# The second product of both layers in seven products, and a new start of the attention stage

## The chip, the cores and the metric

The kernel runs on one NeuronCore of a Trainium2 chip, as one program. It uses five engines: TensorE (PE: matmuls; PEld is its weight load), VectorE (DVE), ScalarE (ACT), GpSimd (POOL) and SyncE (SP, which issues the DMAs). The metric is the device time of one execution in microseconds (us), the median of several runs, less is better. All arithmetic is float32; a matmul operand x is split in a rounded part hi (type fp32r) and a remainder lo = x - hi, and a product is made of three passes: hi·hi, hi·lo, lo·hi.

## What is computed

An attention over chunks of 64 tokens (4 batches, 8 heads, 576 tokens, 64 values per head), and its output through two layers:

```python
x = softmax(q_c @ k_c.T / 8) @ v_c           # in chunks of 64; x: 2304 tokens x 512
h = np.maximum(x @ w_in, 0.0)                # layer one, w_in 512 x 2048
x = (s * (h * h) + b) @ w_out                # w_out 2048 x 512, s and b scalars
h = x @ w2_in                                # layer two, same sizes
y = (np.maximum(h, 0) + np.log1p(np.exp(-np.abs(h)))) @ w2_out
```

The weights arrive as 64-bit floats, and the kernel makes 32-bit floats of them with integer instructions (function `convert`).

## The kernel before, in words

The 2304 tokens are 18 tiles of 128 (two tiles are a unit u, three units a group j; three groups of 768 tokens). Each matrix product is cut in 2 x 2 blocks over rows, columns and tokens. Three of the four big products are then made with seven block products instead of eight (Strassen's scheme in Winograd's form, numbered 1 to 7), for which sums of blocks of weights and of tokens ("forms") are made beforehand. A matmul here is 128 x 128 weights against 384 tokens (N = 384, half a group).

There are five stretches.
- Attention: per tile scores (L815), a maximum, exponentials, their sum, a scaling on POOL (L899), a transpose (L915) and the values (L934). The first `EARLY` = 6 tiles take their exponentials head by head on ACT (eight instructions, L839), the others in one (L874) with a subtraction and a sum on DVE. q, k and v of a tile lie in one of three places. While PE has nothing to do, it runs filler matmuls on zeros (L1502), a number fixed when the program is written.
- First product of layer one: `first_product` runs 24 quads (feature block i of 8, group j of 3), each of seven products of six matmuls (L1000). The products of a quad run through four accumulators in PSUM; between them ACT copies a partial sum to the next accumulator (`seed`, L1022) and DVE adds (L571). `hidden` (L1032) applies the relu on ACT, and the result goes to DRAM. The last two feature blocks come in the order `ENDING`, one after the other.
- Second product of layer one: `block`, six blocks (group, half), with all eight block products (L1179): 16 hidden blocks x 4 output blocks x 3 passes each. The hidden values are loaded again, squared on ACT (L1148), scaled by s and shifted by b (L436, L438), and split (L584, L593).
- First product of layer two: as for layer one, with Softplus; DVE then makes four sums per quad (L1080 to L1083) for the seven products that follow, and all seven forms are stored.
- Second product of layer two: `second_by_blocks`, seven products (L1335), product by product, and inside a product over the groups 2, 0, 1.

The order is set by a planner (`Work.order`): each operation is put down with the engines that may do it, a cost, a due key and what it depends on; the planner simulates the engines and always starts the operation that can start first, by key. A table TUNE shifts the keys. The instructions are emitted in that order, one fixed queue per engine. All DMAs go through SP's queue (`load`). Accumulators and buffers are `Place`s of a few kinds with a fixed number each.

## Time and profile before

| | us |
|---|---|
| median of three timed runs (808.88 to 811.23) | 809.07 |
| span of the profiled execution, first to last instruction | 805.9 |
| PE busy | 797.4 (99%) |
| PEld busy | 780.1 (97%) |
| DVE busy | 637.8 (79%) |
| ACT busy | 510.1 (63%) |
| POOL busy | 140.6 (17%) |
| DMA queue of SP, share of 16 engines' span | 66.9% |

The profiled execution has no time of its own beside its span; the median of the timed runs is 3.2 us longer than the span. Matmuls overlap: the length of one (some 335 ns) is not what it costs; that is the busy time of a full stretch divided by its matmuls. The mean length of a DVE or ACT instruction too includes an end that overlaps the next one's start when the engine has a backlog. The trace's mean granted TensorE clock is 0.999 of the full 2.4 GHz.

### The profile page before, as it was taken

What the parts mean: (1) busy time and instruction counts of PE and PEld (TensorE: products, weight loads), DVE (VectorE), ACT (ScalarE), POOL (GpSimd) and SP (SyncE); (2) the same over time, 40 slices, a digit from 0 to 9 for tenths busy, and PEclk for the clock granted to TensorE, in tenths of its full rate; (3) what the DMA queues carried; (4) which work ended last, traced back from release to release, by engine and by line L of the source; (5) the groups of instructions that cost most, each with busy time, mean ns of one, the idle gap of its engine ahead of it and who ended that gap; (6) DMA issues with size and microseconds to landing.
All of it is one profiled execution on the core that took longest, in us unless ns stands there. A gap on an engine that the chain in (4) does not pass through costs nothing.

```text
span 805.9 us, 14677 instructions
## 1 busy us (share of the span) xinstructions
PE 797.4 (99%) x5191; PEld 780.1 (97%) x5191; DVE 637.8 (79%) x1166; ACT 510.1 (63%) x1085; POOL 140.6 (17%) x162
## 2 busy tenths in 40 slices
PE   8999999999999999999999999999999999999998
PEld 6788999999999999999999999999999999999997
DVE  5999898988868978889946786898865777778864
ACT  5756866666658777776676764655555566555553
POOL 3444411111110112222212320213100000000000
PEclk9999999999999999999999999999999999999999
DMA  8865367878769666777540056766778997678851
GB/s 256 248 179 160 138 210 261 278 245 274 246 227 383 235 202 194 253 222 252 166 136 29 30 191 212 260 227 225 256 261 286 345 347 241 233 236 289 282 176 60
DMA packets 80634, 180.28 MB, mean 224 GB/s; under 512 B 9008, under 2 KB 53040, under 8 KB 79664
## 3 DMA queue, kind: packets, MB, share of 16 engines
q1 hardware_dynamic: 80560, 179.34, 66.9%
q8 instruction: 41, 0.67, 0.4%
q14 instruction: 33, 0.27, 0.1%
HBM read 111.15 MB, written 68.16 MB: 222 GB/s over the span
## 4 chain that ended last, share of the span: by engine, by line
PE 95%; DVE 3%; ACT 1%; issue 0%; POOL 0%; ACTq 0%; POOLq 0%; DVEq 0%
PE at L1000 20%; PE S L1000 13%; PE at L1179 9%; PE S L1179 9%; PE A L1000 9%; PE S L1335 8%; PE at L1335 8%; PE A L1179 6%; PE A L1335 5%; PE S L1502 2%; PE at L934 2%; PE at L815 1%; PE at L915 1%; DVE operands L593 1%; ACT last L839 0%
## 5 line engine op out<-in xcount | busy, mean ns | idle before, releaser
L571 POOL TENSOR_TENSOR mem<-mem 128x256 f32<-128x256 f32 x120 | 104.8, 883 | 377.6 <-DVE mem L551 279.9
L593 DVE TENSOR_TENSOR operands<-mem,operands 128x384 fp32r<-128x384 f32 (+4 forms) x186 | 126.3, 695 | 38.4 <-ACT operands L584 36.8
L593 DVE TENSOR_TENSOR operands<-last,operands 128x384 fp32r<-128x384 f32 (+2 forms) x184 | 111.2, 625 | 46.7 <-ACT operands L584 39.7
L584 ACT CAST operands<-mem 128x384 fp32r<-128x384 f32 (+4 forms) x186 | 111.7, 621 | 55.6 <-PE at L1335 36.0
L584 ACT CAST operands<-last 128x384 fp32r<-128x384 f32 (+2 forms) x184 | 93.5, 528 | 57.8 <-PE S L1179 23.1
L1000 PE MATMUL at<-operands 128*128 128x384 f32 x624 | 120.1, 336 | 0.4 <-ACT S L1022 0.4
L1000 PEld LDWEIGHTS at<-operands 128*128 128x128 f32 x624 | 109.4, 188 | 0.8 <-ACT S L1022 0.7
L1335 PE MATMUL at<-operands 128*128 128x384 f32 x384 | 87.2, 334 | 0.0
L1335 PE MATMUL S<-operands 128*128 128x384 f32 x384 | 87.2, 334 | 0.0
L1179 PE MATMUL at<-operands 128*128 128x384 f32 x432 | 84.5, 335 | 0.9 <-ACT operands L584 0.8
L1000 PE MATMUL S<-operands 128*128 128x384 f32 x420 | 83.6, 336 | 0.0
L1179 PE MATMUL S<-operands 128*128 128x384 f32 x432 | 83.1, 334 | 0.0
L1179 PEld LDWEIGHTS at<-operands 128*128 128x128 f32 x432 | 75.5, 188 | 1.9 <-ACT operands L584 1.1
L1032 ACT ACTIVATE mem<-S 128x384 f32<-128x384 f32 x104 | 51.0, 492 | 38.8 <-PE S L1000 29.3
L1179 PEld LDWEIGHTS S<-operands 128*128 128x128 f32 x432 | 75.6, 188 | 0.0
L1000 PEld LDWEIGHTS S<-operands 128*128 128x128 f32 x420 | 73.6, 188 | 0.3 <-issue 0.2
L571 DVE TENSOR_TENSOR mem<-mem 128x384 f32<-128x384 f32 (+1 forms) x108 | 61.0, 573 | 14.3 <-ACT mem L1032 10.8
L1335 PEld LDWEIGHTS S<-operands 128*128 128x128 f32 x384 | 68.4, 188 | 0.0
L1335 PEld LDWEIGHTS at<-operands 128*128 128x128 f32 x384 | 68.4, 188 | 0.0
L1000 PE MATMUL at<-last,operands 128*128 128x384 f32 x336 | 65.7, 335 | 0.0
L1000 PE MATMUL A<-operands 128*128 128x384 f32 x300 | 60.2, 339 | 0.4 <-DVE A L571 0.4
L1000 PEld LDWEIGHTS at<-last,operands 128*128 128x128 f32 x336 | 58.8, 188 | 0.0
(80 smaller groups left out, 1226.1 us busy)
## 6 DMA issues: line engine op xcount, KB each, us to landing
mem<-in_w_dram SPq DMA_DIRECT2D x64, 512.0 KB, 4.6
summed<-mem SPq DMA_DIRECT2D x168, 192.0 KB, 2.5
mem<-summed SPq DMA_DIRECT2D x30, 768.0 KB, 5.5
hid<-mem SPq DMA_DIRECT2D x96, 192.0 KB, 3.0
...
```

What stands on the lines that cost most here:

```text
L571: lambda e: on(e).tensor_tensor(out=out(), in0=x(), in1=y(), op=op or ALU.subtract),
L584: lambda e: nc.scalar.copy(out=hi().bitcast(F32R), in_=x()),
L593: lambda e: nc.vector.tensor_tensor(out=lo().bitcast(F32R), in0=x(), in1=hi(), op=ALU.subtract),
L815: nc.tensor.matmul(out_[c * D : (c + 1) * D, pr], of("q")[:, pr * P + c * D : pr * P + (c + 1) * D], kb[:, :, pr, c, :], start=True, stop= ...
L915: nc.tensor.transpose(at(pt)[:, c], of("e")[:, c], ident)
L934: nc.tensor.matmul(at(px)[y, x], of("v")[y, x], of("aT")[y, x], start=True, stop=True)
L1000: nc.tensor.matmul(acc(dst)().rearrange("p (u c) -> p u c", u=GROUP), l[a], r[c], start=start and kk == 0 and x == 0, stop=kk == 1 and x == 2,
L1032: lambda e: nc.scalar.activation(out=at(go), in_=acc(place)(), func=AF.Softplus if ph else AF.Relu),
L1179: nc.tensor.matmul(at(accs[d])[:, :N], l[a], r[c], start=m == 0 and z == 0, stop=m == NM - 1 and z == 2,)
L1335: nc.tensor.matmul(at(accs[d])[:, :N], l[a], r[c], start=i == 0 and y == 0, stop=i == NF - 1 and y == 2,)
L1502: nc.tensor.matmul(x, nought, nought.unsqueeze(1).to_broadcast([P, KK, P]), start=True, stop=True)
```

## The change

The second product of layer one is made in seven products too, by the same function as that of layer two (`second`), with the token groups outermost (2, 0, 1) and the products 1, 5, 6, 3, 7, 2, 4 inside a group. Four of the products run on in the accumulators of an earlier one (`GOES_ON`). Three of seven need sums of stored features; these are now made by DVE from loaded chunks, four feature blocks at a time (`summed_up`, 1536 elements per partition), in both layers, so that a quad stores four forms instead of seven (`FOUR`). The square moves to the quads (`squared`: ACT, or DVE straight from PSUM); s is applied when a result is read from PSUM, and b as a bias, b times the column sums of the weights, which come from two extra columns in three of the 21 steps of layer one. The weights' sums for the second product are made by POOL in `weights2` in both layers. All seven sets of weights are split once, during group 2, and kept in the SBUF.

In `convert`, layer one and the first weights of layer two take the sign and exponent through ACT (two Prelu instructions instead of one Relu; the first step on ACT or DVE) instead of one DVE instruction. The first six tiles of q, k and v have a place each, loads of the first four may be issued from ACT's queue, tiles 0, 1 and 3 alone take the head-by-head exponentials. The last two feature blocks are interleaved by group in both layers (`ENDING`). TUNE, some of the planner's costs and some keys change with it.

```diff
-EARLY = 6
+ENDING = [(i, j) for j in (2, 0, 1) for i in (NF - 2, NF - 1)]
+
...
+ORDER = 1, 5, 6, 3, 7, 2, 4
+GROUPS = 2, 0, 1
...
+GOES_ON = {2: 1, 3: 5, 7: 6, 4: 7}
+STAGE = 8, 7, 6, 5, 4, 3, *(8, 7, 6) * 4
+SLOTS = {"b": (3, 4), "t": (0, 1), "v": (2, 5), "u": (2, 5)}
+FIRST = SLOTS | {"b": (6, 7), "v": (3, 4)}
+GH, NGH = 896, 4
...
-            {"SP": 0.45},
+            {"SP": 0.55, "ACT": 0.6} if early else {"SP": 0.5},
             key,
-            lambda e: nc.sync.dma_start(out=out(), in_=in_()),
+            lambda e: (nc.scalar if e == "ACT" else nc.sync).dma_start(out=out(), in_=in_()),
...
+        leaky = ph == 0 or part == 0 and c < 4
...
+            elif e == "ACT":
+                nc.scalar.activation(
+                    out=a().bitcast(I32), in_=top(), func=AF.Identity, scale=1.0 / 16, bias=-15.0 / 32
+                )
...
+        o2 = add({"ACT": act(DM)}, key, scaled, [o1], [am])
+        o5 = add(
+            {"ACT": act(DM)} if leaky else {"DVE": dve(DM)}, key, signed, [o2], [am] if leaky else [f, am]
+        )
...
+        for o, l, r, op in ((4, 1, 3, ALU.add), (1, 0, 1, None), (5, 4, 0, None), (6, 2, 5, None)):
...
-        a = AT_X2 + t % 3 * XS
+        if t == 6:
+            another_use(2)
...
-        sc, pt, px = Place("at"), Place("at"), Place("at")
+        sc, pt, px = Place("A" if t < 6 else "at"), Place("at"), Place("at")
...
-            out_ = lambda: hid[ph][2 * j + half][:, 2 * i + row]
-            st = load(key + 0.1, out_, lambda: at(go), P * N * 4, [o], [go])
-            hid_in.setdefault((ph, j, half), []).append(st)
+
+            def squared(e):
+                if e == "DVE":
+                    nc.vector.tensor_tensor(out=at(go), in0=at(go), in1=acc(place)(), op=ALU.mult)
+                else:
+                    nc.scalar.activation(out=at(go), in_=at(go), func=AF.Square)
+
+            return go, add({"ACT": act(N), "DVE": dve(N, port=False)}, key, squared, [o], [place, go])
+
...
+        if FOUR[ph]:
+            o1 = sub(key, of(b12), of(b12), of(b11), N, [b12[1], b11[1]], [b12[0], b11[0]])
...
-    def block(ph, j, half, t0, first):
...
-            g, src = lambda x=x: mem(*x, 2 + 2 * ph), [ld]
-            if ph == 0:
-                o = add(
-                    {"ACT": act(N)},
-                    key - LEAD_H,
-                    lambda e, g=g: nc.scalar.activation(out=g(), in_=g(), func=AF.Square),
-                    [ld],
-                    w=[x],
-                )
...
-            for d in range(4):
...
-                    for z, (a, c) in enumerate(((0, 0), (0, 1), (1, 0))):
-                        nc.tensor.matmul(
...
-    def second_by_blocks(ph, t0):
...
+    def second(ph, t0):
...
+        steps = [(n, j) for j in GROUPS for n in ORDER]
...
+        summing = {(1, g0), (2, g0), (5, g0)} if ph == 0 else set()
...
+        def summed_up(x, y, z, key):
+
+            a, b, c = [(CHUNKS[w], CHUNK) for w in (x, y, z)]
+            sub(key, lambda: here(*a), lambda: here(*b), lambda: here(*c), CHUNK, (), r=[b, c], w=[a])
...
+
+                    def more(e, ps=ps, y=y):
+                        if ph:
+                            nc.vector.tensor_tensor(out=y(), in0=ps(), in1=y(), op=ALU.add)
+                        else:
+                            nc.vector.scalar_tensor_tensor(
+                                out=y(), in0=ps(), scalar=s_sb[:, 0:1], in1=y(), op0=ALU.mult, op1=ALU.add
+                            )
...
+                        elif e == "ACT":
+                            nc.scalar.activation(
+                                out=y(), in_=ps(), func=AF.Identity, scale=s_sb[:, 0:1], bias=bias[:, c : c + 1]
+                            )
...
+            if n in (1, 5, 6):
+                accs[n, j] = [Place({1: "at", 5: "A", 6: "S"}[n]) for d in range(2)]
+            else:
+                accs[n, j] = accs[{2: 1, 3: 5, 7: 6, 4: 6}[n], j]
...
+            if n == 1:
+                for x, m, ahead in (("b", 1, 0), ("t", 5, 3), ("v", 3, 6)):
+                    for h in range(2):
+                        chunk(place[x][h], m, j, h, t + ahead + h * 4 * T - LEAD_G - 8 * (j == g0))
+            elif n == 7:
+                for h in range(2):
+                    chunk(place["u"][h], 2, j, h, t + (5 + h * 4) * T - LEAD_G)
...
+                b, tt, v, u = [place[x][h] for x in "btvu"]
+                if n == 6:
+                    summed_up(tt, v, tt, th - LEAD_H - 3)
+                elif n == 7:
+                    summed_up(b, tt, b, th - LEAD_H - 5)
+                elif n == 4:
+                    summed_up(u, u, tt, th - LEAD_H - 8)
+                slots.append(CHUNKS[{1: b, 5: tt, 6: tt, 2: u, 7: b, 3: v, 4: u}[n]])
+            more = 2 if (n, j) in summing else 0
...
-                                at(accs[d])[:, :N],
+                                at(p[d])[:, : N + more],
                                 l[a],
                                 r[c],
-                                start=i == 0 and y == 0,
+                                start=n in (1, 5) and i == 0 and y == 0,
...
-                    [*parts, *v2_ready[n, i], *([o] if i else [])],
-                    [wp, *accs],
-                    r=[hi, lo, *([apart] if i == 7 else [])],
+                    [*parts, *ready[n, i], *([o] if i else [*seeds, *seen.get((GOES_ON.get(n), j), ())])],
...
+    def all_products(ph, times, t0, key_w, kinds, early=None):
+        order = [(0, 0), (1, 0), (0, 1), (1, 1), (0, 2), (1, 2)]
+        order += [(i, j) for i in range(2, NF - 2) for j in range(NG)] + ENDING
...
+    t0, sets_done = second(0, end)
...
+    second(1, end)
```

On PE, at the start of layer one's second product, before (A, S and at are accumulators in PSUM, operands lies in SBUF; x6 is six matmuls that follow each other):

```order
L1000 MATMUL at_70<-operands 128x384 x6
L1000 MATMUL S_67<-operands 128x384 x6
L1000 MATMUL A_66<-operands 128x384 x6
L1179 MATMUL at_71<-operands 128x384 x3
L1179 MATMUL A_65<-operands 128x384 x3
L1179 MATMUL S_69<-operands 128x384 x3
L1179 MATMUL S_68<-operands 128x384 x3
L1179 MATMUL A_65<-operands 128x384 x6
```

The same place on PE after the change (shared_1_2653 holds the split features, shared_1_600 the tokens' forms of group 1):

```order
L1097 MATMUL S_67<-operands 128x384 x6
L1097 MATMUL S_68<-shared_1_600,operands 128x384 x6
L1097 MATMUL at_71<-shared_1_600,operands 128x384 x6
L1490 MATMUL at_72<-shared_1_2653,operands 128x386 x3
L1490 MATMUL at_70<-shared_1_2653,operands 128x386 x3
L1490 MATMUL at_72<-shared_1_2653,operands 128x386 x3
L1490 MATMUL at_70<-shared_1_2653,operands 128x386 x3
L1097 MATMUL A_65<-shared_1_600,operands 128x384 x6
L1490 MATMUL at_72<-shared_1_2653,operands 128x386 x3
```

Four accumulators took turns in a block; now one product fills two accumulators, its first two feature blocks stand ahead of the last product of the quads, and its matmuls have 386 columns in this group.

On DVE, in the first products of that stretch, before (L593 splits features, 384 wide, or weights, 512 wide; L438 scales; L479 to L551 convert weights of layer two; last holds features):

```order
L593 TENSOR_TENSOR operands<-last_2621,operands 128x512
L438 TENSOR_SCALAR last_2621<-last_2621,s_sb,b_sb 128x384
L593 TENSOR_TENSOR operands<-last_2621,operands 128x384 x2
L593 TENSOR_TENSOR operands<-last_2621,operands 128x512
L479 TENSOR_SCALAR mem<-mem 128x512
L593 TENSOR_TENSOR operands<-last_2621,operands 128x384
L509 TENSOR_SCALAR mem<-mem 128x512
```

DVE there after the change (L673 splits features, 384, and weights, 2x256; L650 makes a sum of chunks; shared_2 and mem hold chunks):

```order
L673 TENSOR_TENSOR shared_1_2653<-shared_2_2667,shared_1_2653 128x384
L650 TENSOR_TENSOR shared_2_2667<-mem,shared_2_2667 128x1536
L650 TENSOR_TENSOR mem<-shared_2_2667,mem 128x1536
L673 TENSOR_TENSOR shared_1_2653<-shared_2_2667,shared_1_2653 128x384 x2
L650 TENSOR_TENSOR shared_2_2667<-mem,shared_2_2667 128x1536
L673 TENSOR_TENSOR shared_1_2653<-shared_2_2667,shared_1_2653 128x384 x3
L1351 TENSOR_SCALAR bias<-A_66,b_sb 128x1
L1351 TENSOR_SCALAR bias<-A_65,b_sb 128x1
L673 TENSOR_TENSOR operands<-mem,operands 128x2x256 x2
```

Scalings and conversions are gone from between the splits; sums of 1536 elements and the splits of a whole set of weights per product stand there instead.

On ACT, in the first product of layer one, before (L1032 relu, L1022 the copy to the next accumulator, L429 another copy out of PSUM, L496 a step of `convert`, L584 a split):

```order
L1032 ACTIVATE mem<-S_69 128x384
L1022 COPY S_69<-A_65 128x384
L429 COPY mem<-A_66 128x384
L1032 ACTIVATE mem<-S_68 128x384
L496 ACTIVATE mem<-mem 128x512
L1032 ACTIVATE mem<-A_65 128x384
L1032 ACTIVATE mem<-S_69 128x384
L1022 COPY S_69<-A_66 128x384
```

ACT there after the change (L1131 relu, L1145 the square, L1120 the copy to the next accumulator, L479 another copy, L663 a split):

```order
L1131 ACTIVATE mem<-S_69 128x384
L479 COPY mem<-A_66 128x384
L1145 ACTIVATE mem<-mem 128x384
L663 CAST shared_1_1223<-mem 128x512
L1131 ACTIVATE mem<-S_68 128x384
L1120 COPY S_67<-A_66 128x384
L663 CAST shared_1_1223<-mem 128x512
L1131 ACTIVATE mem<-S_67 128x384
L1145 ACTIVATE mem<-mem 128x384
L1131 ACTIVATE mem<-A_66 128x384
```

After most relus a square now stands ahead of the next copy to an accumulator.

## Rows read from the trace of the kernel before

**Rows 1.** The page's first lines: busy time, share of the span, instructions.

```profile
span 805.9 us, 14677 instructions
PE 797.4 (99%) x5191; PEld 780.1 (97%) x5191; DVE 637.8 (79%) x1166; ACT 510.1 (63%) x1085; POOL 140.6 (17%) x162
```

**Rows 2.** Busy time by stretch; the first row names the columns.

```profile
core 0: us, PE busy (x) PEld busy (x) DVE busy (x) ACT busy (x) POOL busy (x), PEclk, DMA share, GB/s
0.00:50.00 50.00, 47.49 (x577) 36.85 (x578) 39.43 (x86) 31.45 (x125) 21.63 (x31) 1.00 0.86 244
50.00:247.50 197.50, 197.16 (x1439) 192.65 (x1440) 169.26 (x302) 130.58 (x254) 47.54 (x53) 1.00 0.68 226
247.50:255.00 7.50, 6.57 (x37) 5.99 (x36) 7.50 (x16) 7.50 (x18) 0.00 (x0) 1.00 1.04 400
255.00:450.60 195.60, 195.59 (x1128) 195.22 (x1127) 157.56 (x283) 139.13 (x284) 41.51 (x46) 1.00 0.57 187
450.60:628.00 177.40, 176.62 (x1014) 175.79 (x1014) 138.22 (x247) 105.08 (x216) 29.89 (x32) 1.00 0.67 228
628.00:801.00 173.00, 173.00 (x1000) 172.95 (x999) 124.71 (x237) 96.34 (x191) 0.00 (x0) 1.00 0.73 249
801.00:806.00 5.00, 0.96 (x6) 0.64 (x4) 1.08 (x2) 0.00 (x0) 0.00 (x0) 0.89 0.23 80
```

**Rows 3.** Fillers in the chain that ended last: start us, us, what.

```profile
4.73 2.82 PE S L1502 x9
8.57 1.82 PE S L1502 x7
```

**Rows 4.** DVE instructions by line and shape: count | busy, mean ns | idle before.

```profile
L593 DVE TENSOR_TENSOR operands<-last,operands 128x384 fp32r<-128x384 f32 x144 | 84.1, 601 | 35.7 <-ACT operands L584 34.7
L593 DVE TENSOR_TENSOR operands<-mem,operands 128x384 fp32r<-128x384 f32 x120 | 66.0, 555 | 32.4 <-ACT operands L584 31.1 <-DMA mem<-summed 0.5
L593 DVE TENSOR_TENSOR operands<-mem,operands 128x512 fp32r<-128x512 f32 x14 | 9.6, 688 | 0.0
L593 DVE TENSOR_TENSOR operands<-mem,operands 128x1024 fp32r<-128x1024 f32 x22 | 26.7, 1216 | 0.9 <-ACT operands L584 0.9
L571 DVE TENSOR_TENSOR mem<-mem 128x384 f32<-128x384 f32 x96 | 55.7, 587 | 12.1 <-ACT mem L1032 10.8
L537 DVE SCALAR_TENSOR_TENSOR mem<-mem 128x512 uint32<-128x512 uint32 x64 | 45.6, 712 | 1.4 <-ACT mem L496 1.4
L551 DVE SCALAR_TENSOR_TENSOR mem<-mem 128x512 f32<-128x512 f32 x64 | 44.6, 696 | 1.3
L523 DVE SCALAR_TENSOR_TENSOR mem<-mem 128x512 f32<-128x512 uint32 x64 | 44.4, 694 | 0.9
L509 DVE TENSOR_SCALAR mem<-mem 128x512 uint32<-128x512 uint32 x64 | 32.0, 501 | 0.0
L479 DVE TENSOR_SCALAR mem<-mem 128x512 uint32<-128x512 uint32 x64 | 31.5, 492 | 10.6 <-DMA mem<-in_w_dram 9.6
```

**Rows 5.** ACT instructions by line and shape, same columns.

```profile
L1148 ACT ACTIVATE last<-last 128x384 f32<-128x384 f32 x96 | 45.5, 515 | 2.9 <-DMA last<-hid 2.9
L496 ACT ACTIVATE mem<-mem 128x512 int32<-128x512 int32 x64 | 40.5, 634 | 28.9 <-DVE mem L479 28.5
L1022 ACT COPY S<-at 128x384 f32<-128x384 f32 x80 | 37.4, 468 | 23.5 <-PE at L1000 21.2 <-DVE mem L571 0.6 <-DVE mem L523 0.6
```

**Rows 6.** In order of time, engines with a backlog: start us, us of the run.

```profile
326.74 1.76 ACT L1148 ACTIVATE last<-last 128x384 f32<-128x384 f32 x4
712.38 2.42 DVE L593 TENSOR_TENSOR operands<-mem,operands 128x384 fp32r<-128x384 f32 x5
```

**Rows 7.** POOL's sums by line, and one beside DVE in order of time.

```profile
L571 POOL TENSOR_TENSOR mem<-mem 128x256 f32<-128x256 f32 x120 | 104.8, 883 | 377.6 <-DVE mem L551 279.9 <-ACT mem L429 22.8 <-ACT S L1022 14.6
302.88 0.98 POOL L571 TENSOR_TENSOR mem<-mem 128x256 f32<-128x256 f32 x1 [8.27 <-DVE mem L551]
303.19 0.96 DVE L479 TENSOR_SCALAR mem<-mem 128x512 uint32<-128x512 uint32 x1
```

931 lines of the change are left out of this document (474 added, 457 removed), and 100 rows, old and new, of the table TUNE.

## The prediction

> **What bounds the kernel now.** Three views were read. First the opening lines of the profile: PE is busy 797.4 of 805.9 us and its weight loads 780.1, while DVE has 79%, ACT 63% and POOL 17% [rows 1]. A busy PE is not yet PE at its peak, so the second view was the busy time by stretch [rows 2]. From 255 to 450.6 us PE runs 1128 matmuls in 195.59 us, 173.4 ns for each; from 628 to 801 us it runs 1000 in 173.00 us, 173.0 ns. These stretches have the same pitch and no hole: PE is the bound there, at the granted clock of 1.00, and DVE (81% and 72% busy) and ACT (71% and 56%) fit beside it. What PE loses lies elsewhere: 0.93 us between 247.5 and 255 us, where DVE and ACT are busy the whole time, 0.78 us between 450.6 and 628 us, 0.34 us between 50 and 247.5 us, the first 2.5 us, and about 4 us at the end, after the last matmul, for a read of PSUM and the last store [rows 2]. The third view, the chain of waits, shows the first 50 us as attention with fillers between: nine in 2.82 us, seven in 1.82 us [rows 3]. The fillers are part of PE's queue and take their time whether PE would have had to wait or not.
>
> So matmuls taken away anywhere after the attention come off the end one for one, as long as DVE and ACT can feed the shorter stretches. That is the whole question.
>
> **The matmuls.** Before, layer one's second product has 6 blocks x 16 hidden blocks x 4 output blocks x 3 passes = 1152 matmuls. After, it has 7 products x 3 groups x 8 feature blocks x 2 x 3 = 1008. The other three big products keep their 1008 each. 144 matmuls go, at 173.4 ns [rows 2]: -25.0 us. Three of the 21 steps have 386 columns instead of 384, that is 144 matmuls with two more each. A filler has 512 columns and costs 1.82/7 = 260 ns [rows 3]; against 173.4 ns for 384 this is 0.68 ns a column, so 288 columns cost +0.2 us. The fillers become 75 instead of 74: +0.3 us. The attention's own matmuls stay as many. PE alone thus gives 805.9 - 25.0 + 0.2 + 0.3 = 781.4 us of span.
>
> The Trainium skill gives a shorter pitch (TensorE: Matmul & The Clock Gate, Back-to-back issue gap): N / 2.4 + 2.5 ns when warm, an estimate of 162.5 ns for N = 384. By it the 144 matmuls would be worth 23.4 us, and the span 1.6 us more; the stretches above do not show that pitch, so their own is used.
>
> **The start.** Six places for q, k and v and a second issuing queue could bring tiles earlier. But the DMA engines already have a share of 0.86 in the first 50 us [rows 2], and the program still carries 14 fillers ahead of the first scores (9 before) and 75 in all. Since PE works through its queue in order, the attention cannot end earlier than the sum of its matmuls and fillers, which is what it was. I take 0; the bounds are -2.5 us (the idle 2.5 us of PE in the first 50) and, if the weights that are now converted earlier crowd DVE, which has 39.43 of the first 50 us, +3 us.
>
> **First product of layer one (50 to 247.5 us).** Squares move here: between the quads' first and last matmul the program has 61 on ACT (5 before) and 31 on DVE. 56 more on ACT at 515 ns make 28.8 us. Conversions: 28 x 2 Prelu instead of 31 Relu, 25 more at 634 ns, 15.9 us; 17 exponent steps on ACT, 10.8 us; copies and splits -2 us [rows 5]. ACT goes from 130.6 to 184 us of 197.5 by mean lengths. With a backlog squares follow each other at (1.76 - 0.515)/3 = 0.415 us [rows 6], 0.8 of the mean; by that pitch the addition is 43 us and ACT stands at 174. So ACT is 88 to 93% busy. DVE gets 21 more subtractions (0.587 us) and 31 squares (taken as the same), +30.5 us, and loses 31 instructions like L537 (0.712), 20 like L479 (0.492) and some ten others: -38 us or more [rows 4]. It eases from 169 to about 160. No engine exceeds PE. What can be late is a copy to the next accumulator (L1120), behind which PE's next product waits, since it now stands behind squares in ACT's queue. One ACT instruction is half a product of PE (6 x 173 ns = 1.04 us), and two quads take turns. Before, with DVE at 86%, this stretch cost PE 0.34 us in all. Bounds: 0, and 48 copies late by one 0.468 us instruction, 22 us. I take +0.5, near the row of before, since no sum passes the stretch.
>
> **Second product of layer one (PE needs 1008 x 173.4 ns = 174.8 us).** DVE is the engine to watch. It has 168 splits of 384, 18 sums of 1536, some 30 splits of 512, 26 reads of PSUM, four conversions and some 24 others. No 1536-wide instruction is in the trace: from 512 to 1024 elements a split grows from 0.688 to 1.216 us [rows 4], so the same step again gives 1.74 us by mean length, and 1.65 us if 0.09 us overlaps. Upper end, all by the longest means (0.601, 1.74, 0.688, 0.587, 1.89 per conversion, 0.6): 101 + 31 + 21 + 15 + 8 + 14 = 190 us. Lower end, by the backlog pitch (2.42 - 0.555)/4 = 0.466 us per split [rows 6] and others scaled alike: 78 + 30 + 18 + 12 + 7 + 12 = 157 us. A DVE that has a backlog works by pitch, so I take 160, 92% of the stretch. In group 2, where all weights are split too, the program puts more in than PE's time in two or three products: about 27 us of DVE by pitch beside 25 us of PE. Before, such a place at the same point (DVE busy 7.50 of 7.50 us) cost PE 0.93 us [rows 2]. I take +1.5 us. ACT is lighter than before: squares and scalings are gone. DMA: 24 chunk loads as before, fewer others, at a share of 0.57 [rows 2].
>
> **Layer two.** First product: DVE loses 69 subtractions at 0.587 us (-40.5) and gains 18 conversions at 0.712 + 0.696 + 0.694 + 0.501 + 0.492 = 3.1 us (+55.7), and some splits: 138.2 becomes about 156 of 177.4 us [rows 2, 4]; nothing is charged but +0.3 us. Second product: the same 1008 matmuls; DVE gets 18 sums and loses as many adds of 384, 133 to 153 us of 173: +0.2 us at group 2. The end: the last read is a copy instead of an addition, 0.
>
> **Sum.** 781.4 + 0 + 0.5 + 1.5 + 0.3 + 0.2, less 0.5 because the hole at 247.5 us lies where new ones are charged: 783.4 us of span. The median of the runs is 3.2 us over the profiled span, and with this the forecast is 786.6, said as 786.5 us.
>
> **Rivals.**
> - No new waits, and the holes of 0.93 and 0.78 us go as well, because group 2 now ends two quads earlier and the last quad is interleaved with the first features: 781.4 - 1.7 + 3.2 = 783 us. For it: DVE at 81 to 86% never starved PE in a full stretch [rows 2]. Against it: 92% now.
> - DVE sets the pace of layer one's second product. If instructions cost their means, it needs up to 190 us against 174.8: +15 at most, +8 in the middle: 793 us, at most 800. For it: a split took 0.601 us on average in this stretch before, 0.555 us in the last stretch, where POOL is idle [rows 2, 4]. Against it: POOL has 14 sums in this stretch instead of 46, and means count overlap twice.
> - POOL holds DVE up in layer two's first product, which now has 68 POOL sums instead of 32. In the trace a DVE step that normally takes 0.492 us took 0.96 us while a POOL sum ran from 302.88 to 303.86 us [rows 4, 7]. If each of the 36 more keeps DVE for its 883 ns, 156 + 32 = 188 us stand against 177.4: +10, 796 us. The Trainium skill has this as a rule (SBUF — State Buffer, Who interferes with whom): DVE and GpSimd share a port pair under an exclusive lock, and the loser blocks for the whole instruction. The trace agrees in that row; most POOL sums, though, find DVE in an operation that does not collide or wait themselves.
> - Slower than before: copies to the next accumulator arrive late in layer one's first product, because ACT's queue is at 88 to 93%. There are 24 quads x 2 = 48 such copies. The gain of 25 us is gone when each makes PE wait 0.52 us, about one ACT instruction; at 0.7 us each the time is 816 us. For it: ACT's load rises by a third there. Against it: two quads alternate, and the sum still leaves 7%.
>
> **How the numbers follow.** The forecast of 786.5 (783.5 to 790) has 0.50, the first rival 0.20, DVE's pace 0.17, POOL's port 0.08, the late copies 0.05. 0.3% is 2.4 us, about what can be told from no change here. All but the last lie over 10 us below 809.07, and a mild form of the last does too: faster 0.95, same 0.01, slower 0.04. The range leaves out half of the first rival's low side and the upper tails: 780 to 796 us.
>
> **What would show it.** In the new profile: 1008 matmuls in layer one's second product at 173 ns, over some 175 us without a hole beyond its first three products; ACT at 88 to 93% in the first product of layer one with PE holes under 1 us in sum; DVE about 160 us in the second product; the first product of layer one beginning near 50 us and ending near 247 us. The forecast is wrong if PE waits in many small pieces for ACT copies (L1120) or DVE splits (L673), or if the quads end well off 247 us.

## The result: 813.3 us, slower by half a per cent

The changed kernel takes 813.26 us (median of 6 runs, 811.45 to 814.87), the kernel before beside it 808.98 (807.59 to 811.23): a ratio of 1.0052, 95% interval 1.0036 to 1.0069. The forecast was 786.5. The profiled execution spans 811.7 us, 5.8 more than the one before.

The head of the page after, to be read against [rows 1]:

```profile
span 811.7 us, 14262 instructions
PE 785.0 (97%) x5048; PEld 759.4 (94%) x5048; DVE 675.7 (83%) x1161; ACT 554.2 (68%) x1142; POOL 177.1 (22%) x200
```

There are 143 matmuls fewer (5191 to 5048: 144 gone, one filler more), but PE's busy time fell by 12.4 us only, where these matmuls were 25 us; and PE is idle for more of a longer span.

The busy time by stage, cut where the stages of the changed kernel begin, beside [rows 2]:

```profile
0.00:55.00 55.00, 49.80 (x594) 39.45 (x595) 41.70 (x87) 33.63 (x92) 26.55 (x38) 0.97 0.77 231
55.00:263.50 208.50, 202.24 (x1436) 192.88 (x1436) 169.17 (x300) 178.72 (x361) 73.66 (x80) 1.00 0.72 235
263.50:453.00 189.50, 183.58 (x1029) 180.57 (x1027) 169.15 (x288) 124.43 (x251) 14.86 (x15) 0.98 0.40 134
453.00:632.00 179.00, 174.77 (x1000) 172.79 (x999) 154.59 (x258) 115.20 (x233) 62.07 (x68) 1.00 0.76 256
632.00:808.00 176.00, 174.36 (x996) 173.75 (x994) 140.54 (x230) 101.97 (x209) 0.00 (x0) 0.99 0.42 142
```

PE has lost time in every row. The forecast of the other engines' load came out: ACT 178.72 us in layer one's first product (174 to 184 was said), DVE 169.15 in its second (157 to 190), both less than the stretch. Over a whole stage, then, load was not the limit.

For an exact ledger the 384- and 386-column matmuls were counted in the trace, and the start of the first of each quarter taken as the stage's border (the 1st, 1009th, 2017th and 3025th after; before, 144 more in the second quarter). Lengths in us:

| stage | before | after | forecast change | measured change |
|---|---|---|---|---|
| up to the first product | 49.8 | 55.1 | +0.3 | +5.2 |
| layer one, first product | 200.1 | 207.6 | +0.5 | +7.5 |
| layer one, second product | 200.5 | 186.2 | -23.8 | -14.3 |
| layer two, first product | 176.6 | 180.7 | +0.3 | +4.1 |
| layer two, second product and end | 178.8 | 182.1 | +0.2 | +3.3 |
| span | 805.9 | 811.7 | -22.5 | +5.8 |

So 28.3 us were missed, in five places. The rows for each follow.

**The start.** ACT's queue after, with its DMA issues (ACTq):

```profile
0.78 0.40 ACTq L487 DMA_DIRECT2D shared<-in_q_dram  x1
1.21 0.54 ACTq L487 DMA_DIRECT2D shared<-in_k_dram  x1
1.78 1.07 ACTq L487 DMA_DIRECT2D shared<-in_q_dram  x2
5.14 4.10 ACTq L487 DMA_DIRECT2D shared<-in_k_dram  x3
9.69 0.33 ACTq L487 DMA_DIRECT2D shared<-in_q_dram  x1
10.45 0.47 ACTq L487 DMA_DIRECT2D shared<-in_k_dram  x1
10.97 0.63 ACT L556 ACTIVATE mem<-mem 128x512 f32<-128x512 int32 x1 [8.95 <-DMA s_sb<-in_s_dram]
```

The first four issues of this queue take 0.4 to 0.54 us each; three from 5.14 us on take 4.10, and ACT's first compute instruction stands behind all nine. (The profile names the load of s, s_sb, as what ended its wait; in the run without these issues, below, the same instruction starts at 5.29 us, 5 us before that load lands.) In the kernel before it starts 4 us earlier:

```profile
6.96 0.63 ACT L496 ACTIVATE mem<-mem 128x512 int32<-128x512 int32 x1 [4.94 <-DVE mem L479]
```

After the change DVE, which works in order, waits for ACT's second step, and PE for the exponentials of the first tile:

```profile
12.30 0.69 DVE L630 SCALAR_TENSOR_TENSOR mem<-mem 128x512 f32<-128x512 f32 x1 [5.09 <-ACT mem L575]
17.44 0.91 PE L908 MATMUL A<-shared 128*64 128x128 f32 x6 [2.89 <-ACT shared L932]
```

**The start of layer one's second product**, in group 2, where all weights have to be split too. The third product's weights (ACT L663 of 768 columns), the sums of 1536 (DVE L650), the splits of features (L663, L673 of 384), and PE, lines left out between:

```profile
277.66 1.14 ACT L663 CAST operands<-mem 128x768 fp32r<-128x768 f32 x2 [2.55 <-DMA mem<-forms]
278.53 1.29 DVE L673 TENSOR_TENSOR operands<-mem,operands 128x768 fp32r<-128x768 f32 x2 [2.53 <-ACT operands L663]
280.21 1.75 DVE L650 TENSOR_TENSOR shared<-mem,shared 128x1536 f32<-128x1536 f32 x1
280.35 1.15 PE L1490 MATMUL A<-shared,operands 128*128 128x386 f32 x5 [0.63 <-DVE shared L673]
282.00 1.76 DVE L650 TENSOR_TENSOR mem<-shared,mem 128x1536 f32<-128x1536 f32 x1
282.07 1.75 ACT L663 CAST shared<-shared 128x384 fp32r<-128x384 f32 x4 [2.85 <-DVE shared L650]
282.64 0.44 PE L1490 MATMUL S<-shared,operands 128*128 128x384 f32 x1 [1.14 <-ACT shared L663]
283.67 1.02 DVE L673 TENSOR_TENSOR shared<-shared,shared 128x384 fp32r<-128x384 f32 x2
284.28 1.01 PE L1490 MATMUL S<-shared,operands 128*128 128x384 f32 x2 [1.20 <-DVE shared L673]
```

First ACT and DVE stand idle for 2.5 us, for weights that the DMA engines bring late; then two sums, of which only the first is needed now, keep the splits back. The table by stretch tells what came of it (the columns are those of [rows 2]; the clock is the third number from the end):

```profile
272.00:276.00 4.00, 4.00 (x25) 4.00 (x24) 3.94 (x8) 3.09 (x7) 0.00 (x0) 1.00 0.85 303
276.00:280.00 4.00, 3.19 (x17) 2.61 (x15) 1.47 (x3) 1.55 (x3) 0.00 (x0) 1.00 1.01 392
280.00:284.00 4.00, 1.59 (x6) 1.02 (x6) 3.96 (x4) 1.75 (x4) 0.00 (x0) 0.95 0.78 279
284.00:288.00 4.00, 3.41 (x9) 2.90 (x10) 4.00 (x9) 1.53 (x3) 0.00 (x0) 0.50 0.03 10
288.00:292.00 4.00, 4.00 (x18) 4.00 (x18) 3.79 (x6) 2.39 (x6) 0.00 (x0) 0.69 0.37 104
```

The granted clock falls from 2.4 to 1.2 GHz behind the holes. Between 288 and 292 us PE is "busy" all the time and counts 18 matmuls, where from 272 to 276 us it counts 25.

**The first product.** One of its small waits, PE's steps and the copy between them:

```profile
105.75 1.33 PE L1097 MATMUL A<-shared,operands 128*128 128x384 f32 x6
107.12 0.46 ACT L1120 COPY S<-A 128x384 f32<-128x384 f32 x1
107.64 1.16 PE L1097 MATMUL S<-shared,operands 128*128 128x384 f32 x5 [0.55 <-ACT S L1120]
```

ACT begins the copy 0.04 us after the product has ended: it is not late. PE's own order has nothing between the product and the one that needs its copy. Of the eight waits over 0.1 us from 100 to 200 us three are of this kind (0.55, 0.55 and 0.66 us, the last one for an addition of DVE); in the other five, 1.5 us together, the awaited copy or addition stands behind other work of ACT or DVE. From 100 to 200 us this adds up; before first, then after:

```profile
100.00:200.00 100.00, 100.00 (x578) 100.00 (x577) 88.95 (x153) 65.51 (x128) 16.56 (x20) 1.00 0.77 254
```

```profile
100.00:200.00 100.00, 96.67 (x538) 92.38 (x538) 86.26 (x143) 89.98 (x182) 37.34 (x43) 1.00 0.71 235
```

Forty matmuls fewer are 6.9 us at 173.4 ns, of which the busy time shows 3.3: each restart costs more than the idle time beside it. At 107.64 us a matmul starts 0.89 us after the one before it, and the next one 0.28 us later, where 0.173 us is usual: a hole of 0.55 us costs 0.83.

The stage has a second part. Up to 100 us PE also works on the last attention tiles, and waits for their steps on ACT (a copy, L479) and DVE (a subtraction, L955):

```profile
72.45 1.09 PE L908 MATMUL at<-shared 128*64 128x128 f32 x16 [0.68 <-ACT shared L479]
75.60 1.09 PE L908 MATMUL at<-shared 128*64 128x128 f32 x16 [0.98 <-DVE shared L955]
```

Five such waits are 2.8 of the 6.3 us of idle time of the stage; before, the whole stage had 0.34 us [rows 2]. DVE, which is busy for 81% of the stage, is busy for 19.76 of the 20 us from 55 to 75 us.

### The profile page after: what moved, and what is told of

Read it like the earlier page. It is cut to its first block, busy times and chain, and to the rows that moved or that the text cites. A ratio compares the mean times of both kernels' runs of the same rounds, so it can differ in the third digit from the quotient of the medians.

```text
span 811.7 us, 14262 instructions
## 1 busy us (share of the span) xinstructions
PE 785.0 (97%) x5048; PEld 759.4 (94%) x5048; DVE 675.7 (83%) x1161; ACT 554.2 (68%) x1142; POOL 177.1 (22%) x200
## 4 chain that ended last, share of the span: by engine, by line
PE 75%; DVE 12%; ACT 6%; DMA 4%; issue 2%; ACTq 0%; DVEq 0%
PE at L1097 16%; PE S L1490 16%; PE at L1490 10%; PE S L1097 10%; PE A L1490 8%; PE A L1097 7%; DVE shared L673 4%; DMA mem<-forms 2%; DVE operands L673 2%; PE at L1028 2%; PE S L1615 2%; DVE mem L650 2%; PE at L908 1%; ACT mem L1131 1%; DVE shared L650 1%
## 5 line engine op out<-in xcount | busy, mean ns | idle before, releaser
L673 DVE TENSOR_TENSOR shared<-mem,shared 128x384 fp32r<-128x384 f32 (+3 forms) x225 | 129.2, 597 | 35.9 <-ACT shared L663 35.1
L663 ACT CAST shared<-mem 128x384 fp32r<-128x384 f32 (+2 forms) x225 | 115.9, 534 | 58.5 <-PE S L1490 23.6
L663 ACT CAST shared<-shared 128x384 fp32r<-128x384 f32 (+1 forms) x172 | 87.4, 517 | 71.3 <-PE S L1490 23.4
L650 POOL TENSOR_TENSOR mem<-mem 128x256 f32<-128x256 f32 x88 | 77.5, 900 | 242.6 <-DVE mem L630 209.8
L1097 PE MATMUL at<-shared,operands 128*128 128x384 f32 x648 | 126.1, 335 | 2.5 <-ACT S L1120 2.2
L1097 PEld LDWEIGHTS at<-shared,operands 128*128 128x128 f32 x648 | 113.2, 188 | 3.8 <-ACT S L1120 2.8
L650 POOL TENSOR_TENSOR shared<-shared 128x256 f32<-128x256 f32 x76 | 69.6, 932 | 168.8 <-PE S L1490 76.8
L673 DVE TENSOR_TENSOR shared<-shared,shared 128x384 fp32r<-128x384 f32 (+2 forms) x172 | 92.7, 567 | 15.0 <-ACT shared L663 14.8
L1490 PE MATMUL A<-shared,operands 128*128 128x384 f32 (+1 forms) x540 | 96.8, 335 | 1.2 <-DVE shared L673 0.6
L1490 PEld LDWEIGHTS A<-shared,operands 128*128 128x128 f32 x540 | 93.9, 188 | 1.8 <-DVE shared L673 0.9
L1490 PE MATMUL S<-shared,operands 128*128 128x384 f32 x432 | 83.1, 348 | 5.3 <-DVE shared L673 3.1
L1490 PEld LDWEIGHTS S<-shared,operands 128*128 128x128 f32 x432 | 79.0, 197 | 7.6 <-DVE shared L673 4.4
L1097 PE MATMUL S<-shared,operands 128*128 128x384 f32 x414 | 82.6, 337 | 2.3 <-ACT S L1120 1.5
L1097 PEld LDWEIGHTS S<-shared,operands 128*128 128x128 f32 x414 | 72.1, 188 | 4.6 <-ACT S L1120 2.8
L673 DVE TENSOR_TENSOR operands<-mem,operands 128x512 fp32r<-128x512 f32 (+3 forms) x69 | 64.7, 953 | 7.5 <-ACT operands L663 7.5
L1131 ACT ACTIVATE mem<-S 128x384 f32<-128x384 f32 x104 | 51.0, 491 | 26.5 <-PE S L1097 24.5
L1097 PE MATMUL at<-operands 128*128 128x384 f32 x312 | 61.2, 335 | 0.7 <-ACT mem L479 0.7
L663 ACT CAST operands<-mem 128x512 fp32r<-128x512 f32 (+3 forms) x69 | 53.6, 796 | 7.7 <-DMA mem<-forms 3.1
L1097 PEld LDWEIGHTS at<-operands 128*128 128x128 f32 x312 | 54.6, 188 | 1.1 <-ACT mem L479 1.0
```

Of the source, the lines that this page charges most:

```text
L650: lambda e: on(e).tensor_tensor(out=out(), in0=x(), in1=y(), op=op or ALU.subtract),
L663: lambda e: nc.scalar.copy(out=hi().bitcast(F32R), in_=x()),
L673: lambda e: nc.vector.tensor_tensor(out=lo().bitcast(F32R), in0=x(), in1=hi(), op=ALU.subtract),
L1097: nc.tensor.matmul(acc(dst)().rearrange("p (u c) -> p u c", u=GROUP), l[a], r[c], start=start and kk == 0 and x == 0, stop=kk == 1 and x == 2,
L1131: lambda e: nc.scalar.activation(out=at(go), in_=acc(place)(), func=AF.Softplus if ph else AF.Relu),
L1490: nc.tensor.matmul(at(p[d])[:, : N + more], l[a], r[c], start=n in (1, 5) and i == 0 and y == 0, stop=i == NF - 1 and y == 2, skip_group_c ...
```

## The experiments

Fifteen kernels ran, five rounds each. All keep the planner's order unless it says otherwise; what changes is the instruction that is issued at a place, so that one cost at a time is taken away. "Short" means that an instruction does a few columns and the rest of its work is left out. "Stages" are lengths as in the ledger. Each ratio is to the kernel before, timed beside the run; the runs were made in four groups, and between groups the ratios are to be compared. In the edits `...` stands for what is left out.

**All loads on SyncE.**

```
-lambda e: (nc.scalar if e == "ACT" else nc.sync).dma_start(...)
+lambda e: nc.sync.dma_start(...)
```

> The changed kernel in the same order, except that all loads of q and k are issued by SyncE; the nine that ScalarE issued in the first 11 us go to SyncE's queue at their places in the order. Theory: ScalarE stood behind its own load issues from 2.0 to 10.97 us (8.95 us without a compute instruction), VectorE waited 5.09 us for it and TensorE 2.89 us at 14.54 us; with these issues gone the hole and the lower clock behind it go, the first product of layer one begins 3 to 5 us earlier than at 55.05 us, and the time is 808.5 to 811 against 813.3. Rival: the loads are late because the DMA engines are full in the first 20 us, whoever issues them; then the first product still begins near 55 us and the time stays at 812.5 to 814.

807.65 us, ratio to before 0.999 (0.9977 to 1.0003), 0.85 us below the theory's range; the first product begins at 50.5 us. ACT's first compute instruction comes at 5.29 in place of 10.97 us:

```profile
5.29 0.63 ACT L556 ACTIVATE mem<-mem 128x512 f32<-128x512 int32 x1 [3.27 <-DVE mem L536]
```

The issues on ACT cost 4.5 of the 5.2 us that the start lost. The stages after it are as long as before this edit, but for the second product (183.9), whose stretch at the lower clock was 3.4 us in place of 6.8. The kernel is then as fast as the one before, and no faster.

**The control: the same issues in the kernel before.**

```
-lambda e: nc.sync.dma_start(...)
+lambda e: (nc.scalar if early else nc.sync).dma_start(...)
...
+early=t < 3,
```

The last line stands at the load of q and at those of k.

> One part of the change alone, in the kernel before and in its order: the nine loads of q and k of the first three tiles are issued by ScalarE in place of SyncE. Theory: load issues wait in ScalarE's queue for the DMA queues, and its first conversions and exponentials wait behind them; ScalarE's first compute instruction, at 6.96 us before, comes at 9 us or later, and the time is 810 to 814 against 808.4. Rival: it took the six places and the other order to make the start late; the issues alone cost nothing or bring the tiles earlier: 806.5 to 809.

813.93 us, 1.0066 (1.005 to 1.0082). ACT's queue:

```profile
5.33 2.64 ACTq L446 DMA_DIRECT2D last<-in_k_dram  x2
9.26 2.74 ACTq L446 DMA_DIRECT2D last<-in_k_dram  x2
12.05 0.63 ACT L496 ACTIVATE mem<-mem 128x512 int32<-128x512 int32 x1 [10.03 <-DMA last<-in_k_dram]
```

One part of the change, put alone into the old kernel, makes it as slow as the change did. Here the tiles come late too, and PE's scores wait for k:

```profile
14.01 1.09 PE L816 MATMUL at<-last 128*64 128x128 f32 x16 [2.43 <-DMA last<-in_k_dram]
```

What slows the issues themselves is not shown; in the run on SyncE three loads of k from 5.52 us on were issued in 1.88 us.

**Short sums.**

```
-sub(key, lambda: here(*a), lambda: here(*b), lambda: here(*c), CHUNK, ...)
+short = lambda x: here(*x)[:, :8]
+sub(key, lambda: short(a), lambda: short(b), lambda: short(c), CHUNK, ...)
```

> The changed kernel in the same order; the 36 sums of 1536 columns on VectorE (18 in each second product) do only 8 columns, so most of the sums of kept products are left out. Theory: the PE holes at 282 to 284, 439.6 and 646 to 648.5 us (1.14, 1.20, 1.08, 1.07 and 0.57 us) stand behind two such sums of 1.75 us each in VectorE's queue, and the granted clock falls to the lower level behind the first and the last of these places (6.8 and 3.4 us long, half of it lost). Then 5 us of holes and up to 5 us of clock go: 803 to 807. Rival: the sums only stand where the DMA engines (379 to 418 GB/s from 264 to 285 us) bring the weights late; then the holes stay, the clock falls as before, and the time is 811 to 813.

807.96 us, 0.9993 (0.998 to 1.0007), above the range of the theory; its execution had a start of 57.4 us. The second products' stages say more: 180.2 in place of 186.2 and 180.1 of 182.1, with no stretch at the lower clock in either. Of the six holes over 0.5 us in layer one's second product two are left (0.51 and 1.03 us); in layer two's that of 0.57 went and that of 1.07 stayed (1.01). Against the 183.9 us of a later run whose clock stayed up as well (every sum by itself), the sums are 3.7 us of layer one's second product; against the 182.0 of the run with zeros, whose clock stayed up there too, 1.8.

**Short squares.**

```
+x = at(go)[:, :8]
...
-nc.scalar.activation(out=at(go), in_=at(go), func=AF.Square)
+nc.scalar.activation(out=x, in_=x, func=AF.Square)
```

The square on DVE is cut in the same way.

> The changed kernel in the same order; the squares in layer one's first product do only 8 of 384 columns (61 on ScalarE, 31 on VectorE), so most of the squares are left out. Rival of the prediction: the copies to the next accumulator are late because squares stand ahead of them in ScalarE's queue. Between 100 and 200 us PE ran 543 matmuls where before it ran 583, which is 6.9 us; if the squares do it, most of that comes back: 806 to 808. Theory: PE waits there because its order puts a product right behind the copy that it needs, with nothing else ready between (a copy of 0.46 us and two hand-overs, 0.5 us each), so that shorter squares give back 0 to 2.5 us: 811 to 813.

810.76 us, 1.0024 (1.0013 to 1.0035), 0.24 us below the theory's range. 550 matmuls from 100 to 200 us in place of 538, and 205.2 us for the first product: 2.4 of its 7.5 us. Of the waits from 100 to 200 us the three whose copy or addition is not late stay (0.55, 0.55, 0.66), and the others shrink from 1.5 to 0.55 us together. The squares in the queues (61 of 92 are ACT's) are a third of the stage's loss: so much of the prediction's last rival is true.

**Sums and weight splits later.**

```
+for ph in range(2):
+    first = [f"second{ph}{x} 6 2 0/1" for x in range(2)]
+    if ph == 0:
+        later([f"set0 6/{x}" for x in (6, 7, 8, 9)], first)
+    later([f"load{ph} 7 2/{x}" for x in (2, 3)], [f"second{ph}{x} 6 2 1/1" for x in range(2)])
```

`later(names, behind)` puts the named operations behind the last of the others: the weight splits of the third product's second half behind its first feature splits, and two sums behind its last.

> The changed kernel with the whole work and the same order except for group 2 of the two second products: the two sums for the fifth product of the group go behind the splits of the third product, which until then stand behind them, and in layer one the weight splits of the third product's second half go behind its first four feature splits. Theory: 1.7 us goes from the holes at 646 to 648.5 us and 2.5 to 3.5 us from those at 279 to 287 us, and if the holes become short enough the clock doesn't fall either (up to 5 us more): 804 to 810. Rival: the weights and chunks land too late for the third product in any order (the DMA engines move 379 to 418 GB/s there); then the wait only changes its name, 811.5 to 813.5.

816.47 us, above both ranges. It tells nothing of the sums: moved there, the weight splits stood behind the load that refills their buffer (ACT waits 0.78 us for it at 286.62 us), so by this order the third product used the next set's weights in its second half.

**Sums later, loads on SyncE.** The same without the weight splits, and one sum of the last group behind four splits.

> The whole work. As the run with all loads on SyncE (807.65 us), and in group 2 of both second products the two sums for the fifth product go behind the third product's splits in VectorE's queue; one more sum of the last group of layer one, which stood straight behind another, goes behind four splits. Theory: VectorE's order sets these waits. Of the holes that the run on SyncE had at 275 to 280 us (0.87, 1.20 and 1.29), 432.7 (1.07) and 639.7 to 641.8 us (1.07 and 0.58), about 5 us go, and the clock that fell to the lower level at 280.4 and 642.3 us (3.4 us each) stays up, 3.4 us more: 799 to 803. Rival: weights and chunks come late from the DMA engines, so that another wait ends last: 806 to 808.

809.58 us, 1.0007 (0.999 to 1.0024), above both ranges: no better than without (0.999). The hole of 0.58 us in layer two went and one of 1.52 came at 655 us, where the two moved sums now stood in a row; the holes at 275 to 280 us stayed, for the third product's own second sum was still between its splits.

**Zeros in the holes.**

```
+fill = {'second00 6 2 0/2': [9], 'second01 6 2 0/2': [5], 'second10 6 2 0/2': [6]}
...
+if op.on == "PE" and fill.get(getattr(op, "own", None)):
+    for x in range(fill[op.own].pop(0)):
+        spare(op)
```

`spare` is a matmul on zeros into a free bank S.

> The whole work. As the run with all loads on SyncE (807.65 us), and at three places in group 2 of the second products, where TensorE waits, it gets matmuls on zeros into a bank of PSUM that is free: 9 and 5 ahead of the third product's first two steps in layer one, 6 ahead of the first in layer two (about 1.9, 1.1 and 1.3 us of work; the idle times there are 2.07, 1.29 and 1.65 us). No wait gets shorter. Theory: the holes bring the granted clock down at 280.4 and 642.3 us; filled, the clock stays at its upper level, and up to half of 6.8 us comes back: 804 to 806, with no stretch at the lower level between 20 and 800 us. Rival: the clock falls there for another reason; then it falls again and the time stays at 807 to 808.5.

805.9 us, 0.9975 (0.996 to 0.999). Where the run on SyncE, first, had a clock of 0.57, this one has 1.00:

```profile
276.00:280.00 4.00, 1.76 (x7) 1.19 (x7) 4.00 (x5) 1.35 (x5) 0.00 (x0) 1.00 0.65 264
280.00:284.00 4.00, 3.66 (x12) 3.66 (x13) 3.86 (x9) 2.56 (x5) 0.00 (x0) 0.57 0.16 18
```

```profile
276.00:280.00 4.00, 3.94 (x18) 2.85 (x16) 4.00 (x6) 1.36 (x4) 0.00 (x0) 1.00 0.43 169
280.00:284.00 4.00, 3.91 (x22) 3.91 (x23) 4.00 (x9) 3.97 (x9) 0.00 (x0) 1.00 0.17 18
484.00:488.00 4.00, 3.17 (x11) 3.17 (x12) 2.84 (x5) 1.47 (x3) 3.54 (x4) 0.64 0.56 180
```

No work of the other engines became shorter, and the second products did (182.0 and 180.6 in place of 183.9 and 182.1). But the clock fell at 485 us, behind the unfilled hole of 2.16 us in layer two's first product. Behind the same hole it fell in the profiles with short sums, short squares and sums later too, and not in those of the change and of the run on SyncE: a hole of this size can bring it down and need not.

**Short conversions.** On the run with SyncE.

```
+cut = 8 if ph == 0 and part == 1 else DM
...
+a = lambda: at(am)[:, :cut].bitcast(U32)
```

> As the run with all loads on SyncE (807.65 us), in the same order; the conversions of layer one's second weights (sixteen, which the change begins 40 us earlier) do 8 of 512 columns in all steps but the last, so that most of that conversion is left out. VectorE gets about 25 us back in layer one's first product, ScalarE about 18. Theory: from 100 to 200 us TensorE loses 6.6 us by its order, in which a product stands right behind the copy it needs with nothing else ready: it loses at least 4.5 us there still, and the time is 804.5 to 807. Rival: it loses them because VectorE and ScalarE are full; then at most 2 us are lost there, and the time is 801 to 803.5.

807.77 us (803.71 to 808.52), 0.998 (0.9969 to 0.9992). 546 matmuls from 100 to 200 us where the run on SyncE has 541: less than 1 us comes back there, and 1.3 us in the whole first product (206.3), though DVE has 75.5 in place of 84.5 us to do and ACT 81.7 in place of 89.7. The loss, still over 5 us, is the theory's. The time lies above both ranges, and why is not shown.

**Every sum by itself.** On the run with SyncE.

```
+for ph in range(2):
+    later(f"load{ph} 6 2/3", splits(ph, 6, 2, 0))
+    later(f"load{ph} 7 2/2", splits(ph, 6, 2, 1))
+    later(f"load{ph} 7 2/3", splits(ph, 3, 2, 0))
+later("load0 4 1/1", splits(0, 4, 1, 0), 2)
```

> The whole work. As the run with all loads on SyncE (807.65 us); in group 2 of both second products every sum of 1536 columns stands by itself in VectorE's queue, the third product's second sum behind its first four splits, the fifth product's first sum behind the third product's last split and its second one four or more splits later (the run that moved both to one place met a new hole of 1.52 us at 655 us, for two sums in a row). Theory: the holes of 1.29 us at 279 us and 0.58 at 641 us go, no new one over 0.7 us comes, and the holes of 0.63 to 1.2 us ahead of the third product's first step stay, since its weights and its chunk come late: 804 to 806.5. Rival: whatever VectorE does first there, something else is late by as much: 807 to 810.

807.51 us, 0.9982 (0.9973 to 0.9991), against 0.999 (0.9977 to 1.0003): nothing that can be told, although the clock stayed up in this profile. The second product takes 183.9 us as without. The rival holds: DVE has as much to do there in any order, and the new holes (0.61 at 283, 0.82 at 293 us, 1.13 at 276) add up to the old ones: 5.3 us of idle time in the stage, 5.4 without, now in more and smaller pieces.

**The same with zeros.** Seven, four and eight ahead of the steps that wait.

> The whole work. As the run in which every sum stands by itself, and matmuls on zeros fill what waits are left: 7 and 4 ahead of the third product's first step in layer one and two, and 8 in layer two's first product where TensorE stood idle for 2.16 us at 482.7 us and the clock fell behind it in the last run with zeros. Theory: the granted clock stays at its upper level from 20 to 795 us, 1.7 to 3.4 us better than the same order without zeros: 801.5 to 804.5. Rival: the clock falls at some other place, and the time is within 1 us of the same order without zeros.

807.57 us, 0.9982 (0.9971 to 0.9994): the clock stayed up, but it had stayed up without, and zeros longer than their hole cost time (1.78 us of them where 1.14 us had been idle; the second product takes 184.8 us). The rival again.

**Short copies.** On the run with SyncE.

```
-nc.scalar.copy(out=acc(place)(), in_=acc(ba)())
+nc.scalar.copy(out=acc(place)()[:, :8], in_=acc(ba)()[:, :8])
```

> As the run with all loads on SyncE, in the same order; the copies to the next accumulator do 8 of 384 columns (96 copies of 0.46 us), so what the accumulators add up is left incomplete. Theory: PE's order has a product right behind the copy that it needs, so each hole of 0.83 us (idle time and restart) in layer one's first product is the copy and two hand-overs; shorter copies take 0.3 to 0.35 us off each of some 12 holes there and off five in layer two: the loss from 100 to 200 us falls from 6.6 to 2.5 to 4 us and the time to 803 to 805.5. Rival: the accumulators come free late, and the copy itself costs nothing: the loss stays over 5.5 us and the time at 807 to 808.

804.36 us, 0.9946 (0.9927 to 0.9965). 553 matmuls from 100 to 200 us (541 with whole copies), 205.1 us for the first product: 2.5 us, and the time is the theory's. The two waits of 0.55 us are 0.24 now and stand at the same places: the order sets where PE waits, and the copy's length how long. It is not the load that counts: short conversions took 8.0 us in 100 off ACT and gave 1.3 us, short copies 5.4 and gave 2.5. The loss from 100 to 200 us is 4.3 us, a little more than the 2.5 to 4 that were expected.

**Short weight sets.** On the run in which every sum stands by itself.

```
-lambda f=f: at(f),
-lambda h=h: forms2[ph][:, W2_AT[n], 4 * h : 4 * h + 4].rearrange("p a b -> p (a b)"),
+lambda f=f: at(f)[:, :256],
+lambda h=h: forms2[ph][:, W2_AT[n], 4 * h],
```

> As the run in which every sum stands by itself; the loads of the second weights' sets bring 256 of 1024 columns each (a quarter of 14 MB in both layers), so the products use old values for the rest. Theory: what is left of the holes at the start of the second products (0.63 us at 275, 0.85 to 1.04 us near 297 us) is the DMA engines, which move 379 to 418 GB/s there; with a quarter of the bytes these go and 1.5 to 3 us, up to 3.4 us more where the clock doesn't fall: 800.5 to 804. Rival: the loads are in time, and ScalarE and VectorE are late with the splits: within 1 us of the same order with whole loads.

804.88 us, 0.9948 (0.9932 to 0.9964), 0.9 us above the theory's range. The second product takes 182.0 us in place of 183.9: late weights are 1.9 us of it. The hole at 276 us goes, that at 291 (0.80) doesn't.

**All of it short at once.** On the run with SyncE: the sums, squares, copies, weight sets and conversions of the runs above.

> As the run with all loads on SyncE, in the same order for every engine, all of TensorE's work kept; at once short: the sums, the squares and the copies to the next accumulator (8 columns each), the weight sets (256 of 1024 columns) and layer one's second-weight conversions (8 of 512 columns in all steps but the last). Most of that work is left out. Theory: the matmuls are worth what was predicted and the loss is what the other engines and the DMA engines make PE wait, added up: the single runs gave 2 to 4 us each, so 791 to 797, with at most 8 us of PE idle time between 3 and 795 us. Rival: PE's order keeps its holes with any speed of the others: 799 or more.

792.77 us, 0.9803 (0.9786 to 0.9821), with 8.5 us of idle time (8 at most were expected; the time is the theory's). Layer one's second product by itself:

```profile
253.70:429.00 175.30, 175.30 (x1009) 175.01 (x1008) 138.77 (x280) 120.55 (x244) 13.96 (x14) 1.00 0.35 119
```

PE runs 1009 matmuls in 175.30 us without a hole. The stages are 50.1, 203.6, 175.5, 179.7 and 180.0: the second product has the 25 us that the matmuls were worth, and the first keeps 3.5 us over the kernel before, layer two's first 3.1, layer two's second 1.2, which none of these edits took away. Of the idle time that is left, 2.7 us are the waits for steps of the last attention tiles at 61 to 71 us, 1.85 the wait for one copy in layer two's first product (473 us) and 1.0 that at the start of its second (627 us); these steps were left whole.

**Zeros in a fourth hole.** As the run with zeros in three, and `"quad1 1 2/7": [8]`.

> The whole work. As the run with loads on SyncE and matmuls on zeros at three places (805.9 us), with 8 more ahead of the product that waits 2.16 us at 482.7 us in layer two's first product, behind which the clock fell at 485.1 us in that run. Theory: no stretch at the lower clock between 20 and 795 us, and 0.5 to 2 us better: 804 to 805.5. Rival: zeros there cost as much as the clock, 805.5 to 807.5.

804.92 us (803.95 to 807.04), 0.9959 (0.9946 to 0.9971): the best with the whole work, 0.4% better than the kernel before and by the two ratios some 0.9% better than the change; from the run with zeros in three (0.9975, 0.996 to 0.999) it can hardly be told. There is no stretch at the lower clock between 20 and 795 us, and the place where it fell in that run has 1.00:

```profile
484.00:488.00 4.00, 3.69 (x19) 3.03 (x18) 3.63 (x6) 1.60 (x5) 3.62 (x3) 1.00 0.54 183
```

**Twelve sums on GpSimd.**

```
+nc.gpsimd.tensor_tensor(out=here(*a), in0=here(*b), in1=here(*c), op=ALU.subtract)
```

> The whole work. As the run with loads on SyncE and zeros at four places; the twelve 1536-column sums for the fifth product of each group are computed by GpSimd in place of VectorE (by the 883 ns of its 256-column sums, an estimate of 5.3 us each, needed some 15 us later). Theory: VectorE sets the waits at the start of group 2; 1.7 us go from the third product's waits in each layer, and the time is 801.5 to 804.5. Rival, the port: VectorE's instructions take longer beside each of GpSimd's sums, by half as in the row of 0.96 us for 0.492, and 12 x 2 us are lost: 808 or more where these waits reach TensorE.

836.17 us, 1.0331 (1.0314 to 1.0348). GpSimd needs 3.67 us for a sum. One of them, the splits on DVE beside it, and PE:

```profile
342.68 5.69 DVE L673 TENSOR_TENSOR shared<-shared,shared 128x384 fp32r<-128x384 f32 x5
342.89 3.65 POOL L1310 TENSOR_TENSOR mem<-shared,mem 128x1536 f32<-128x1536 f32 x1 [5.22 <-ACT shared L663]
347.49 1.69 PE L1494 MATMUL A<-shared,operands 128*128 128x384 f32 x8 [2.62 <-DVE shared L673]
```

Five splits that take 2.4 us alone (0.55 and 0.47 each behind it) take 5.69: the second of them ran 3.71 us, until 0.4 us after GpSimd was done. The port is the rival that the prediction had put in the wrong place: in layer two's first product DVE was busy for 154.59 us in the changed kernel, where 156 were forecast without it and 188 with it.

## Why the prediction was wrong

**The matmuls were right.** 144 of them at 173.4 ns, -25.0 us: with the other engines' work made short, the second product takes 175.5 us against 200.5.

**The start was wrong.** "I take 0", since "the attention cannot end earlier than the sum of its matmuls and fillers". That is a bound from below. Of the moved loads only the DMA engines were looked at, not what stands behind the issues in ACT's queue: a load issue is an instruction of ACT. It measured +4.9 us over the forecast; 4.5 of them go in the run on SyncE, and the control, with the issues alone, loses 5 us.

**Layer one's first product was wrong by 7.0 us.** The step that failed is "I take +0.5, [...] since no sum passes the stretch". The sums were right (ACT 178.72 of 208.5 us), and are no ground for it: PE waits where its order leaves no product between a product and its copy, and where a copy or an addition stands behind other work, and no engine need be full for that. Shown: short copies give 2.5 us, short squares 2.4, short conversions 1.3, and all together 4.0 of 7.5, so that these gains overlap. Most of the rest is the attention's tail, for which the prediction had no term: 2.7 us of idle time there stay with all of it short, 0.34 us before. Why the planner's order has these places now was not tried. The rival of late copies had the right place and a part of the reason: at 107.12 us the copy was not late, behind squares others were. Its time of 816 us (some 818 by its own 48 x 0.7 us) is nearest to the result by luck, for it put some 34 us here, where 7.5 were lost.

**Layer one's second product was wrong by 9.5 us.** The +1.5 us for group 2 had the place, but was sized from a hole of 0.93 us beside a busy DVE. Short sums, together with a clock that stayed up, give 6.0; short weight sets 1.9; the clock alone is up to half of the 6.8 us. DMA was let pass for its mean share ([rows 2]); at this place the engines move 392 GB/s (276 to 280 us). Another order of the sums gave nothing. That "the holes of 0.93 and 0.78 us go as well", the first rival, was wrong for the same reason.

**Layer two was wrong by 6.9 us.** "+0.3" and "+0.2" were charged by mean load again. In the first product five waits hold 4.2 us of idle time (0.78 before), which with the restarts is its loss. In the longest a weight split stands ahead of an addition on DVE; a copy waits for the addition, and PE for the copy:

```profile
491.67 0.95 DVE L673 TENSOR_TENSOR operands<-mem,operands 128x768 fp32r<-128x768 f32 x1
492.54 0.55 DVE L650 TENSOR_TENSOR mem<-at,mem 128x384 f32<-128x384 f32 x1
493.12 0.46 ACT L1120 COPY S<-at 128x384 f32<-128x384 f32 x1 [0.95 <-DVE mem L650]
493.64 0.62 PE L1097 MATMUL at<-shared,operands 128*128 128x384 f32 x2 [2.16 <-ACT S L1120]
```

In the second the third product of group 2 waits again, and the clock falls:

```profile
646.00:650.00 4.00, 2.36 (x9) 1.78 (x8) 4.00 (x6) 2.77 (x7) 0.00 (x0) 0.86 0.42 154
650.00:654.00 4.00, 4.00 (x18) 4.00 (x18) 2.80 (x5) 1.61 (x4) 0.00 (x0) 0.72 0.08 14
```

Zeros in both gave 1.6 us in the second product and nothing sure in the first (181.1 against 180.8). What puts these five waits into the first product, some 4 us, was not tried: the cause stays open there.

**The clock was not in the sum at all.** The forecast took a granted clock of 1.00 throughout and so each hole at its own length. In the profile after, the lower level comes behind holes three times (clock 0.97 over the first 55 us, 0.50 at 284 to 288, 0.72 at 650 to 654).

**The step from span to time was wrong by 1.6 us.** The 3.2 us put on the span came from an execution faster than the median. For the profiled execution after, the time is 813.53 us and the span 811.7, and the median lies 1.6 us over this span. So the time misses the forecast by 26.8 us, where the span misses it by 28.3.

**The chances were wrong.** 0.95 for faster came from rivals that were each one mechanism of its own; five stages that each lose 3 to 10 us were no case. The signs it named did tell: the first product ends at 262.7 us in place of 247, and PE waits in many small pieces for L1120 and L673.
